# Attention products in 64x64 tiles of the array, chunks of 64 tokens, and a batch's attention woven beside mixing

## The chip, the cores and the metric

The kernel runs on one core of one Trainium2 chip. The metric is the time of one execution on the device in microseconds. Engines are named as in the profile: PE (TensorE, matrix products; PEld are its weight loads), DVE (VectorE), ACT (ScalarE), POOL (GpSimd), SP (SyncE, which issues most transfers). All arithmetic is in float32; each float32 matmul is two weight loads and two matmuls in the trace.

## The reference

A linear attention with a decaying state (4 batches, 8 heads, 768 tokens, 48 dimensions a head), then an MLP mixer over tokens and channels.

```python
# attention, per batch and head; r, k, v, w: [768, 48], u: [48]
state = 0                                     # [48, 48]
for t in range(768):
    y[t] = r[t] @ (state + outer(u * k[t], v[t]))
    state = w[t][:, None] * state + outer(k[t], v[t])
# bridge: heads side by side, x: [4, 768, 384]
h = relu(x^T @ w_tok1) @ w_tok2               # 768 -> 256 -> 768, over tokens
x = x + h^T
out = x + relu(x @ w_ch1) @ w_ch2             # 384 -> 1536 -> 384, over channels
```

The four weight matrices come as float64 and are converted on the chip from their raw bits.

## The kernel before

**Attention.** Tokens are taken in chunks of T = 128, two chunks to a unit, three units to a batch, 12 units in all. Heads lie in pairs: the d rows of one at partitions 0 to 47, of the other at 64 to 111. A unit's r is held twice (lines 84 and 92), once for each head of the pair with zeros at the other head's rows, so that one matmul with all 128 rows of k gives the products of both heads. Within a chunk the weight of token s for token t is a product of w between them; `levels` (line 173) builds it by blocks of 1, 2, 4, ... 64 tokens, 7 levels. A level is a `gram` (line 194, 8 matmuls of 128x128 into a PSUM tile of two banks) and a `join` (line 201): DVE multiplies the right halves of r, head by head (line 203, 64 partitions x 512), POOL the left halves of k (line 205) and the products of w (line 206), and DVE copies the gram's wanted entries into `pairs` under a mask (line 211). The next level's gram needs the r and k of this join.

`post` (line 222) makes the output of a unit, chunk by chunk: k is transposed (`tokens`, line 230), the term with u is made by a product of r*k with u (`own`, line 237, and line 244 on POOL), the output is accumulated from state and pairs (`result`, line 248, lines 255 and 257), and the state is carried on (`carry`, line 261: matmuls of 128x64, lines 269 to 276). Its PSUM tiles share a tag "a" with two buffers.

**Mixing.** `mixing` (line 286) is a batch's MLP: hidden (line 295, matmuls of 384 columns), back (line 301), turn (transposes, line 307), up (line 315, 256 columns, then ACT's Relu, line 317) and down (line 323, 384 columns, then DVE's addition and the transfer out).

**Weights.** `weights` (line 134) gives 28 pieces; each loads float64 bits, takes one ACT operation (line 149), five DVE operations (lines 150 to 153 and 155) and one POOL addition (line 154).

**Order.** `weave` (line 35) spreads lists of pieces over each other by cost. The loop at line 344 goes over the units: a unit's levels beside the unit before it (`post`) and, in units 1 to 3, a third of the conversions; from unit 4 on, a third of the mixing of the batch before. So batch 0's attention, all conversions and one unit of batch 1 stand ahead of the mixing of batch 0, and the last batch's mixing is alone at the end. This is the order of priority; the program's scheduler may bring forward what is ready (token products of batch 0 run from 76 us on). Loads of a unit are issued by SP (line 89).

Of the kernel before, what the change touches and what calls it, by code (L numbers as in the profile page):

```python
# [14 lines left out]
Abs = mybir.ActivationFunctionType.Abs  # L15
Relu = mybir.ActivationFunctionType.Relu

B, H, S, D = 4, 8, 768, 48
DM = H * D          # model width
T = 128             # tokens per chunk  # L20
C = S // T          # chunks per batch
UC = 2              # chunks per unit of attention work
UB = C // UC        # units per batch
NU = B * UB         # units
A = H // 2          # head pairs; heads 2a and 2a+1 lie at partitions 0 and 64
P = 64
LEVELS = 7          # block sizes 1, 2, ..., 64 halve and join a chunk of 128
COLS = UC * A * T   # columns of a unit: (chunk, pair, token)
DTOK, DCH = 256, 1536
NJ = DCH // 128  # L30
NORMAL = float(np.array(0x38100000, np.uint32).view(np.float32))  # upper word of the float64 2^-126
SEG = 256           # tokens per pass through the channel mixing


def weave(*lists):
    """Pieces (cost, f) of several lists, each list in its order and spread over the whole."""
    keyed = []
    for n, pieces in enumerate(lists):
        total, at = sum(c for c, _ in pieces), 0.0
        for i, (c, f) in enumerate(pieces):  # L40
            keyed.append(((at + c / 2) / total, n, i, f))
            at += c
    for *_, f in sorted(keyed, key=lambda e: e[:3]):
        f()


def cut_in(pieces, n):
    size = -(-len(pieces) // n)
    return [pieces[i * size:(i + 1) * size] for i in range(n)]
# [3 lines left out]
def rwkv6_then_mixer(  # L53
    ctx: ExitStack,
    tc: tile.TileContext,
    rkw: bass.AP,      # [unit, head of the pair, d, (r, k, w), (chunk pair token)]
    v: bass.AP,        # [B, S, DM]
    u: bass.AP,        # [head of the pair, d, pair]
    w_tok1: bass.AP,   # the weights are float64, as raw bits
# [3 lines left out]
    out: bass.AP,      # [B, S, DM]  # L63
):
    """The recurrence by chunks of T tokens: within a chunk, token t takes from an earlier token s
    the weight sum_d r[t, d] k[s, d] prod_{s<j<t} w[j, d]. Each pair s < t is parted by exactly one
    block size b: s lies in the left half and t in the right half of one block of 2b tokens. There
    the product is that of w from the middle to t, taken into r, and from s to the middle, taken
    into k; so only products of w over parts of (s, t) occur, whatever w holds."""
# [7 lines left out]
    xpool = ctx.enter_context(tc.tile_pool(name="xpool", bufs=2))  # L77
    ps_g = ctx.enter_context(tc.tile_pool(name="ps_g", bufs=2, space=bass.MemoryType.PSUM))
    ps_a = ctx.enter_context(tc.tile_pool(name="ps_a", bufs=2, space=bass.MemoryType.PSUM))
    ps_m = ctx.enter_context(tc.tile_pool(name="ps_m", bufs=2, space=bass.MemoryType.PSUM))  # L80

    # ---- the units' tiles: zero between the heads' rows, in r also at the other head's rows, and in
    # the weights of pairs where s >= t ----
    rs = [const.tile([128, 2, COLS], f32, name=f"r{i}") for i in range(3)]
    kws = [const.tile([128, 2, COLS], f32, name=f"kw{i}") for i in range(3)]
    pairs = [const.tile([128, UC, A, 2, T], f32, name=f"pairs{i}") for i in range(2)]
    vs = {}

    def load(i):
        for q in range(2):  # L90
            rows = slice(q * P, q * P + D)
# [6 lines left out]
    for i in range(3):  # L98
        (pool if i else dve).memset(rs[i], 0.0)
        (pool if i else dve).memset(kws[i], 0.0)  # L100
# [292 lines left out]
```

## Time and profile before

| | us |
|---|---|
| median of 3 runs (lowest, highest) | 903.5 (900.65, 904.16) |
| span of the profiled execution | 904.2 |
| PE busy (its matmuls, with overlap taken once) | 793.7, 88% |
| DVE busy | 469.1, 52% |
| POOL busy | 258.6, 29% |
| ACT busy | 104.1, 12% |

The span is that of the profiled execution, from its first to its last instruction; nothing of the run's time lies outside of it that would show beside the median. Busy time is a share over stages with different limits, so it has to be read stage by stage.

### The profile page before, as it was taken

The numbers are of one execution on the slowest core, as the hardware profiler recorded it, in microseconds if no ns is written. First come the engines' busy times: TensorE is split into PE (matmuls) and PEld (weight loads), VectorE is DVE, ScalarE is ACT, GpSimd is POOL, SyncE is SP. The second block draws the span as 40 slices with busy tenths as digits, with TensorE's granted clock in tenths as the row PEclk, the third lists the DMA queues.
The fourth block names the chain that finished last, engine by engine and source line by source line (L and its number), as shares of the span: only waits on it lengthen the run. The fifth ranks groups of instructions, "written<-read, shape, count | busy, mean of one in ns | idle before, by whom it ended". The sixth has DMA issues, their size and how long they took to land.

```text
span 904.2 us, 10421 instructions
## 1 busy us (share of the span) xinstructions
PE 793.7 (88%) x4344; PEld 648.0 (72%) x4344; DVE 469.1 (52%) x520; ACT 104.1 (12%) x249; POOL 258.6 (29%) x267
## 2 busy tenths in 40 slices
PE   2567656676689999999999999999899999999998
PEld 2566556566568997977779978777789886668674
DVE  7688697796786664443676644445656300010000
ACT  0001110110111110100011101000111010022010
POOL 8445435352443243121242431212422100000000
PEclk9976756665689999999999999999999999999999
DMA  9304324232110022001020120010000000000000
GB/s 177 78 25 96 110 75 121 70 87 88 52 36 18 19 53 62 9 9 53 9 53 19 36 67 22 10 53 9 1 1 1 1 18 9 27 1 1 18 9 26
DMA packets 14670, 36.84 MB, mean 41 GB/s; under 512 B 2208, under 2 KB 8352, under 8 KB 13472
## 3 DMA queue, kind: packets, MB, share of 16 engines
q1 hardware_dynamic: 14208, 36.18, 15.7%
q8 instruction: 34, 0.56, 0.3%
q10 hardware_dynamic: 416, 0.00, 0.1%
q14 instruction: 12, 0.10, 0.0%
HBM read 31.46 MB, written 4.72 MB: 40 GB/s over the span
## 4 chain that ended last, share of the span: by engine, by line
PE 76%; DVE 11%; POOL 8%; issue 4%; ACT 0%; POOLq 0%; DVEq 0%; ACTq 0%
PE z_ps L315 21%; PE h_ps L323 21%; PE gram L199 18%; DVE r L203 4%; PE y_ps L257 4%; PE h_ps L295 3%; PE y_ps L255 3%; POOL kw L205 3%; PE h_ps L301 2%; POOL decay L206 2%; PE own_ps L240 2%; POOL low L154 1%; DVE pairs L211 1%; DVE cut L151 1%; PE kv_ps L269 1%
## 5 line engine op out<-in xcount | busy, mean ns | idle before, releaser
L199 PE MATMUL gram<-r,kw 128*128 128x128 f32 x1344 | 210.9, 321 | 89.3 <-DVE r L203 66.7
L199 PEld LDWEIGHTS gram<-r,kw 128*128 128x128 f32 x1344 | 200.6, 232 | 101.3 <-issue 48.6
L203 DVE TENSOR_TENSOR r<-r,decay 64x512 f32<-64x512 f32 x144 | 145.4, 1010 | 124.9 <-PE gram L199 113.8
L315 PE MATMUL z_ps<-xT,wch 128*128 128x256 f32 x864 | 200.9, 386 | 0.0
L205 POOL TENSOR_TENSOR kw<-kw,decay 128x512 f32<-128x512 f32 x72 | 110.1, 1529 | 295.0 <-PE gram L199 294.9
L323 PE MATMUL h_ps<-wch,z 128*128 128x384 f32 x576 | 189.4, 487 | 0.0
L315 PEld LDWEIGHTS z_ps<-xT,wch 128*128 128x128 f32 x864 | 162.3, 193 | 21.0
L323 PEld LDWEIGHTS h_ps<-wch,z 128*128 128x128 f32 x576 | 108.5, 190 | 71.7
L211 DVE COPY_PREDICATED pairs<-mask,gram 128x1024 f32<-128x1024 uint8 x84 | 135.1, 1609 | 2.0
L325 DVE TENSOR_TENSOR o<-x,h_ps 128x384 f32<-128x384 f32 x24 | 13.3, 554 | 190.6 <-PE h_ps L323 190.6
L257 PE MATMUL y_ps<-vt,pairs 128*128 128x48 f32 x384 | 76.9, 297 | 10.1 <-DVE pairs L211 8.0
L317 ACT ACTIVATE z<-z_ps 128x256 f32<-128x256 f32 x144 | 55.3, 384 | 249.8 <-PE z_ps L315 249.8
L257 PEld LDWEIGHTS y_ps<-vt,pairs 128*128 128x128 f32 x384 | 63.5, 215 | 11.0 <-DVE pairs L211 8.3
L255 PE MATMUL y_ps<-state,r 128*128 128x48 f32 x320 | 66.3, 292 | 0.0
L255 PEld LDWEIGHTS y_ps<-state,r 128*128 128x128 f32 x320 | 55.2, 213 | 1.8 <-issue 0.6
L244 POOL TENSOR_TENSOR yd<-vt,own_sb 128x384 f32<-128x384 f32 x24 | 23.6, 982 | 98.5 <-ACT own_sb L242 98.5
L154 POOL TENSOR_TENSOR low<-low,cut 128x384 f32<-128x384 f32 (+1 forms) x28 | 34.3, 1224 | 30.4 <-DVE low L153 30.4
L301 PE MATMUL h_ps<-h,wtok 128*128 128x384 f32 x96 | 38.2, 522 | 1.3 <-DVE x L302 1.3
L295 PE MATMUL h_ps<-x,wtok 128*128 128x384 f32 x96 | 38.1, 544 | 0.0
L203 DVE TENSOR_TENSOR r<-r,kw 64x512 f32<-64x512 f32 x24 | 29.1, 1215 | 16.0 <-PE gram L199 15.6
L205 POOL TENSOR_TENSOR kw<-kw 128x512 f32<-128x512 f32 x12 | 22.5, 1877 | 45.2 <-PE gram L199 20.2
L149 ACT ACTIVATE size<-d 128x384 f32<-128x384 f32 (+1 forms) x28 | 16.9, 604 | 154.5 <-DMA d<-in_w_ch_dram 58.0
(45 smaller groups left out, 422.8 us busy)
## 6 DMA issues: line engine op xcount, KB each, us to landing
kw<-in_rkw_dram SPq DMA_DIRECT2D x24, 384.0 KB, 6.2
vt<-in_v_dram SPq DMA_DIRECT2D x12, 384.0 KB, 3.9
r<-in_rkw_dram SPq DMA_DIRECT2D x24, 192.0 KB, 3.3
d<-in_w_ch_dram SPq DMA_DIRECT2D x9, 512.0 KB, 3.6
d<-in_w_ch_dram SPq DMA_DIRECT2D x12, 384.0 KB, 3.1
out_dram<-o SPq DMA_DIRECT2D x24, 192.0 KB, 1.9
d<-in_w_tok_dram SPq DMA_DIRECT2D x3, 512.0 KB, 11.2
d<-in_w_tok_dram SPq DMA_DIRECT2D x4, 384.0 KB, 3.4
```

What stands on the lines that cost most here:

```text
L154: pool.tensor_add(low, low, cut.bitcast(f32))
L199: pe.matmul(g[:, c, a], k_[:, ts(ca, T)], right[:, :, ts(ca, nb), :], start=True, stop=True)
L203: dve.tensor_mul(right[head[q], q], right[head[q], q], wv[head[q], :, 0].unsqueeze(2).to_broadcast([P, n, b]))
L205: pool.tensor_mul(left, left, wv[:, :, 1].unsqueeze(2).to_broadcast([128, n, b]))
L211: dve.copy_predicated(out=dst, mask=masks[l].unsqueeze(1).to_broadcast([128, x, nb, b]), data=src)
L255: pe.matmul(y[:, ts(h, D)], r_[:, q, ts(c * A + a, T)], state[bt][:, a, :], start=True, stop=False)
L257: pe.matmul(y[:, ts(h, D)], at[:, c, a, q, :], vt[:, c, ts(h, D)], start=(ch == 0), stop=True)
L295: pe.matmul(ps, wtok1[:, c, ts(i, 128)], x[:, c, :], start=(c == 0), stop=(c == C - 1))
L301: pe.matmul(ps, wtok2[:, i, ts(c, 128)], h1[:, i, :], start=(i == 0), stop=(i == DTOK // 128 - 1))
L315: pe.matmul(ps, wch1[:, m, ts(jt, 128)], xT[:, m, ts(s, SEG)], start=(m == 0), stop=(m == DM // 128 - 1))
L317: act.activation(zs[s][:, jt, :], ps, Relu)
L323: pe.matmul(ps, zs[s][:, jt, ts(n, 128)], wch2[:, jt, :], start=(jt == 0), stop=(jt == NJ - 1))
```

## The change

- A chunk is 64 tokens; a unit still has 256, so each 128 tokens are two chunks j = 0, 1, and there are 6 levels instead of 7.
- r is held once ("packed"), like k and w; each has a tile of its own and is loaded by its own transfers.
- Each product of a head and a chunk uses one 64x64 tile of the array: head q gives the rows, chunk j the columns. `fours` issues the four in the order (0,0), (1,1), (1,0), (0,1). A gram is 32 matmuls of 48 rows, 64 columns of weights and 32 streamed columns. The row halves write different banks.
- The term with u goes into the first gram: its streamed columns are 32 of r and 64 of r*u (made by ACT), and the diagonal is copied into the weights. `own` falls away, and so does the addition of `yd`.
- The joins run on DVE alone, over both heads at once (112 partitions), three operations. Levels 4 and 5 are copied out of PSUM by ACT, levels 0 to 3 by DVE under a mask.
- The state is carried by chunks of 64; its PSUM tile and that of the output share one buffer. The output is copied by ACT.
- The conversions' addition moves from POOL to DVE. The conversions of the two channel weights move behind the first batch's attention, woven into the mixing of batch 0.
- Order: batch 0's attention (units 0 to 2) with the token weights' conversion; then, for each batch, its mixing with all of the next batch's attention woven through it; a unit's loads are issued at the end of the post pieces of the unit that held the tiles.

The core of the diff:

```diff
-T = 128             # tokens per chunk
-C = S // T          # chunks per batch
+T = 64
+C = S // 128
+ROWS = P + D
-LEVELS = 7          # block sizes 1, 2, ..., 64 halve and join a chunk of 128
+LEVELS = 6
...
-    rs = [const.tile([128, 2, COLS], f32, name=f"r{i}") for i in range(3)]
-    kws = [const.tile([128, 2, COLS], f32, name=f"kw{i}") for i in range(3)]
+    rs = [const.tile([128, COLS], f32, name=f"r{i}") for i in range(3)]
+    ks = [const.tile([128, COLS], f32, name=f"k{i}") for i in range(3)]
+    ws = [const.tile([128, COLS], f32, name=f"w{i}") for i in range(3)]
+    weights_at = [const.tile([128, 2, UC * A, T], f32, name=f"at{i}") for i in range(3)]
...
-            pool.tensor_add(low, low, cut.bitcast(f32))
+        dve.tensor_add(low, low, cut.bitcast(f32))
...
         def begin():
-            L["rk"] = apool.tile([128, UC, A, T], f32, name="rk")
-            rk = L["rk"].rearrange("p c a t -> p (c a t)")
-            for q in range(2):
-                dve.tensor_mul(rk[head[q]], r_[head[q], q, :], k_[head[q]])
...
+            first = L["first"] = apool.tile([128, UC, A, 2, 96], f32, name="first")
+            r5 = r_.rearrange("p (c a j t) -> p c a j t", c=UC, a=A, j=2)
+            for a in range(A):
+                act.mul(first[:ROWS, :, a, :, 32:], r5[:ROWS, :, a, :, :], u_col[:ROWS, a:a + 1])
+            act.copy(first.rearrange("p c a j t -> p (c a j) t")[:ROWS, :, :32],
+                     r_.rearrange("p (n t two) -> p n t two", t=32, two=2)[:ROWS, :, :, 1])
+
+        def fours(f):
+            for q, j in ((0, 0), (1, 1), (1, 0), (0, 1)):
+                f(q, j, slice(q * P, q * P + D), slice(j * T, (j + 1) * T))
...
+        def gram(l):
+            b = 1 << l
+            right = r_.rearrange("p (n two b) -> p n two b", two=2, b=b)[:, :, 1, :]
+            g = L["g"] = ps_g.tile([128, 2, 512], f32, name="gram")
+            for ca in range(UC * A):
+                fours(lambda q, j, rows, cols: pe.matmul(
+                    g[cols, q, ts(ca, 32)], k_[rows, ds(ca * 128 + j * T, T)],
+                    right[rows, ts(2 * ca + j, 32 // b), :], start=True, stop=True))
+
+        def pick(l):
...
+            if l < 4:
...
+                dve.copy_predicated(
...
+                return
+            g = g.rearrange("p q (x t) -> p q x t", t=32)
+            for p in range(0, 128, 2 * b):
+                n = p % T // (2 * b)
+                act.copy(at[p:p + b, :, :, n * 2 * b + b:(n + 1) * 2 * b], g[p:p + b, :, :, ts(n, b)])
 
+        def join(l, w, new):
...
+            dve.tensor_mul(left, left, wv[:, :, 1].unsqueeze(2).to_broadcast([ROWS, n, b]))
+            dve.tensor_mul(right, right, wv[:, :, 0].unsqueeze(2).to_broadcast([ROWS, n, b]))
+            dve.tensor_mul(new[:ROWS], wv[:, :, 0], wv[:, :, 1])
+
+        def first_block():
+            for c in range(UC):
+                gram0(c)
+            join(0, products[0], products[1])
+            for c in range(UC):
+                pick0(c)
+
+        def block(l):
+            gram(l)
+            join(l, products[l], products[l + 1])
+            pick(l)
...
+        def carry(c):
...
+            kv = ps_a.tile([128, 2, 512], f32, name="kv_ps", tag="a")
             for a in range(A):
+                for j, q in ((0, 0), (1, 1), (0, 1), (1, 0)):
+                    if not (last and j == 1):
+                        pe.matmul(kv[ts(q, P), j, ts(a, D)], L["kT"][ts(j, T), a, ts(q, P)],
+                                  vt[ts(j, T), c, ts(2 * a + q, D)], start=True, stop=True)
...
+        def before(c):
+            ch = half * UC + c
+            y = live[i]["y"] = ps_a.tile([128, 2, 512], f32, name="y_ps", tag="a")
...
+                for q, j in got:
+                    pe.matmul(y[ts(j, T), q, ts(a, D)], r_[q * P:q * P + D, ds((c * A + a) * 128 + j * T, T)],
+                              state[bt, 2 * ch + j][q * P:q * P + D, a, :], start=(a == 0), stop=False,
+                              skip_group_check=True)
...
+        def within(c):
...
+                for q, j in pairs:
+                    pe.matmul(y[ts(j, T), q, ts(a, D)], at[ts(j, T), q, c * A + a, :],
+                              vt[ts(j, T), c, ts(2 * a + q, D)], start=(2 * ch + j == 0 and a == A - 1), stop=a == 0,
+                              skip_group_check=True)
+            act.copy(xs[bt][:, ch, :].rearrange("p (a q e) -> p q a e", a=A, q=2),
+                     y[:, :, :A * D].rearrange("p q (a e) -> p q a e", a=A))
...
+            pieces += [(0.5, lambda c=c: tokens(c)), (0.5, lambda c=c: carry(c)), (0.5, lambda c=c: before(c)),
+                       (1.0, lambda c=c: within(c))]
+        return pieces + [(0.01, lambda: load(i + 3))]
...
+        if bt == 0:
+            pieces, ups[0] = woven(pieces, to1), woven(ups[0], to2)
...
+    emit(woven(levels(0), levels(1), conversion(wtok1, w_tok1, 2, 256)))
+    emit(woven(levels(2), post(0) + post(1), conversion(wtok2, w_tok2, 1, 384)))
+    emit(post(2))
+    for bt in range(B):
+        n = (bt + 1) * UB
+        if n < NU:
+            att = levels(n)
+            for i in range(n, n + UB - 1):
+                att += woven(levels(i + 1), post(i))
+            att += post(n + UB - 1)
+            emit(woven(att, mixing(bt)))
+        else:
+            emit(mixing(bt))
```

## Rows read from the trace of the kernel before

**Rows 1.** The page, part 1: busy us, share of the span, instructions.

```profile
PE 793.7 (88%) x4344; PEld 648.0 (72%) x4344; DVE 469.1 (52%) x520; ACT 104.1 (12%) x249; POOL 258.6 (29%) x267
```

**Rows 2.** Stages: length, busy us of PE, PEld, DVE, ACT, POOL; PE clock; DMA.

```profile
13.00:55.00 42.00, 24.57 (x121) 22.86 (x122) 30.64 (x32) 1.34 (x2) 20.15 (x27) 0.96 0.40 81
55.00:250.00 195.00, 127.71 (x706) 116.75 (x703) 157.64 (x217) 19.98 (x39) 87.40 (x81) 0.66 0.31 84
250.00:432.00 182.00, 178.75 (x1038) 146.32 (x1039) 100.19 (x96) 20.65 (x53) 53.23 (x52) 0.95 0.13 32
432.00:614.00 182.00, 179.68 (x1086) 146.29 (x1085) 98.05 (x92) 21.57 (x55) 52.11 (x52) 1.00 0.14 33
614.00:787.00 173.00, 170.68 (x976) 136.49 (x975) 66.77 (x67) 21.57 (x55) 33.32 (x31) 0.98 0.02 8
787.00:904.00 117.00, 112.13 (x427) 79.05 (x425) 7.21 (x13) 17.69 (x44) 0.00 (x0) 1.00 0.03 12
```

**Rows 3.** The chain that ended last, in order of time: start, us, what.

```profile
76.78 2.56 PE h_ps L295 x4
...
289.94 1.78 PE gram L199 x16
...
807.66 31.08 PE z_ps L315 x144
...
869.76 30.97 PE h_ps L323 x96
```

**Rows 4.** Groups by line, 432 to 614 us: busy, mean ns, idle before.

```profile
L199 PE MATMUL gram<-r,kw 128*128 128x128 f32 x336 | 42.3, 277 | 2.2 <-POOL kw L205 2.0 <-DVE r L203 0.2
...
L235 ACT COPY kT<-kT_ps 128x512 f32<-128x512 f32 x5 | 2.9, 586 | 44.0 <-PE kT_ps L233 43.8
```

**Rows 5.** Busy time of line 269 alone (PE, then PEld), count in flight in brackets.

```profile
292.94:293.00 0.06, 0.04 (x2) 0.05 (x2) 1.00 0.00 0
293.00:293.06 0.06, 0.06 (x4) 0.06 (x4) 1.00 0.00 0
293.06:293.12 0.06, 0.06 (x6) 0.06 (x6) 1.00 0.00 0
...
293.04:293.06 0.02, 0.02 (x4) 0.02 (x4) 1.00 0.00 0
```

**Rows 6.** Timeline of PE around a piece of line 269: start, us, instruction.

```profile
291.56 1.46 PE L315 MATMUL z_ps<-xT,wch 128*128 128x256 f32 x6
292.96 0.67 PE L269 MATMUL kv_ps<-vt,kT 128*64 128x48 f32 x16
293.56 2.86 PE L315 MATMUL z_ps<-xT,wch 128*128 128x256 f32 x12
```

**Rows 7.** Timeline of DVE, with one row of POOL: start, us, instruction.

```profile
59.97 0.69 DVE L203 TENSOR_TENSOR r<-r,kw 64x512 f32<-64x512 f32 x1
67.25 0.41 DVE L152 TENSOR_SCALAR scale<-cut 128x512 uint32<-128x512 uint32 x1
67.59 0.67 DVE L151 SCALAR_TENSOR_TENSOR cut<-d,cut 128x512 uint32<-128x512 uint32 x1
68.94 1.38 POOL L154 TENSOR_TENSOR low<-low,cut 128x512 f32<-128x512 f32 x1 [2.50 <-DVE low L153]
69.23 1.64 DVE L203 TENSOR_TENSOR r<-r,decay 64x512 f32<-64x512 f32 x1
78.39 1.23 DVE L211 COPY_PREDICATED pairs<-mask,gram 128x1024 f32<-128x1024 uint8 x1
666.42 0.34 DVE L276 TENSOR_TENSOR state<-state,kv_ps 128x192 f32<-128x192 f32 x1
672.62 2.45 DVE L211 COPY_PREDICATED pairs<-mask,gram 128x1024 f32<-128x1024 uint8 x1
```

**Rows 8.** Timeline of PE: the first matmuls.

```profile
12.81 3.75 PE L199 MATMUL gram<-r,kw 128*128 128x128 f32 x16 [12.81 <-DMA kw<-in_rkw_dram]
```

## What I expected, before the result was known

> **What bounds the kernel now.** I read the page first: PE is busy 88% of the span [rows 1], which alone does not say where an edit pays. So next the busy time by stage [rows 2]. From 13 us one unit's levels run alone, PE and DVE in turn (DVE busy 30.64 of 42 us, 73%). From 55 to 250 us (the rest of batch 0's attention, the weights' conversion, the first unit of batch 1) PE is busy 65% on a granted clock of 0.66, DVE 81%: this goes at the pace of DVE and of the chain through each unit's levels. From 250 to 787 us three stages follow, each one batch's mixing beside the next batch's attention: PE is busy 178.75 of 182, 179.68 of 182 and 170.68 of 173 us; these are bound by PE alone. From 787 us the last batch's mixing runs alone for 117 us.
>
> Busy time of PE overlaps itself, so the price of a matmul is taken from start to start, in the chain of work [rows 3]: 16 gram matmuls in 1.78 us are 0.111 us each, 144 of the first channel product 0.216, 96 of the second 0.323. (Each float32 matmul is two records in the trace, a weight load and a matmul each; I count records, called steps below.) A mixed stage then adds up, with 36 x 3 x 2 and 6 x 12 x 2 steps by the loops: 216 x 0.216 + 144 x 0.323 + 48 steps of token mixing with the same 384 columns at 0.323 + 18 transposes at 0.11 = 46.6 + 46.5 + 15.5 + 2.0 = 110.6 us of mixing. The 336 gram steps [rows 4] take 37.3 us; the rest of the 182 us, 34 us, are the other attention products and about 4.6 us of gaps. Attention so costs PE (182 - 110.6 - 4.6) / 3 = 22.3 us a unit in a mixed stage, and that is what the change cuts.
>
> **The change on PE.** Counted from the loops, a unit has after the change 6 levels x 32 matmuls x 2 = 384 gram steps (112 before), and 2 chunks x 3 pieces (carry, before, within) x 32 = 192 steps for state and output; 8 transposes stay. So 576 small steps stand against (1344 + 192 + 704 + 320) / 12 = 213 before, from the counts that the same loops give: the steps multiply, and all hangs on the price p of one. Nothing in the trace uses 64x64 tiles. The nearest rows are the state products (line 269), which have 64 columns and alternate between two column halves: in three stretches of 58 ns or so the count of matmuls in flight rises from 2 to 4 to 6 [rows 5], so two steps start per 58 ns, 29 ns a step instead of 111. Each half keeps a pace of its own of 58 ns (a load of half the columns), and the two run side by side. The upper bound for p is 58 ns (no two tiles side by side), the nearest measured price is 29 ns (two), the lower bound 14.5 ns (four tiles, each at its own 58 ns). The change goes through the four tiles in turn, no two of a group of four alike, and puts the two row halves into different banks of the gram's tile, so I expect four to run; I take p = 18 ns, nearer to 14.5 than to 29, the rest being allowance for issuing twice as many steps per time as any row shows. Going from full size to tiles and back is in the same rows: the 6 steps of z from 291.56 should end their turn at 292.86, the next z step starts at 293.56 [rows 6]; 0.70 us less 16 x 29 ns is 0.24 us for a piece. A unit has 12 such pieces. A unit costs PE 576 x 0.018 + 8 x 0.11 + 12 x 0.24 + 0.2 (level 0 has 96 columns instead of 32) = 14.3 us instead of 22.3. A mixed stage becomes 110.6 + 3 x 14.3 + 4.6 = 158 us.
>
> [...]
>
> **The change on DVE, ACT and POOL.** The joins' multiplication of k moves from POOL to DVE. In exchange DVE multiplies both heads at once: 512 elements took 0.69 us alone, and 1.64 us when POOL's addition ran beside it [rows 7]; POOL has only memsets left after, so I take 0.69. A unit on DVE: 6 levels x 2 x 0.69 = 8.3; the products of w of 512, 256, ... 16 elements 1.9 (scaled between 0.69 for 512 and 0.34 for 192, [rows 7]); copies under a mask: 1024 elements took 1.23 us, but 2.45 where blocks are 1 or 2 tokens [rows 7], so level 0 (256 elements at the slow pace and 512 of the diagonal, twice) 2.8, level 1 1.2, levels 2 and 3 0.7 each, 5.4; the state's multiplication and addition, 4 x 2 x 0.34 = 2.7. Sum 18.3 us. The copies of levels 4 and 5, the copy of r with u, and the output copy are now ACT's: some 8 to 10 us a unit, at 0.586 us for 512 elements [rows 4] and less for fewer, 30 us at most beside the 21.6 us that ACT has in a stage of 182 [rows 2]; hidden by PE's 158 us. A conversion of 512 columns is 2 x 0.41 + 4 x 0.68 [rows 7] = 3.6 us with the addition that comes over from POOL, one of 384 about 2.9.
>
> Each unit's loads wait at the end of its post pieces on SP, with the outputs of the mixing queued behind; the next use of the tile is a stage later, so this costs nothing as long as the post pieces aren't late.
>
> **Stage by stage.** Start to the first mixing: unit 3 and the 21 conversions of the channel weights leave this stage. DVE has 3 x 18.3 + 3 x 3.6 + 4 x 2.9 = 77 us. The first gram came at 12.81 us [rows 8]; the new one needs r times u, whose load and five ACT operations put it near 14. At 85% busy (81% in the stage of before, more since two units' levels alternate) 77 us take 91: the stage ends at 105 us (91 if DVE never waits, 120 at 73%).
> First mixed stage: 158 us of PE, but the 21 conversions (9 x 3.6 + 12 x 2.9 = 67 us of DVE) lie in its first third: there DVE has 67 + 33% of 3 x 18.3 + 3 = 88 us against 33 us of mixing and 14 of attention on PE. Attention pieces wait behind conversions on DVE and PE waits with them, up to 40 us; part is filled by mixing products that need neither, as now, where token products run between attention pieces long before their stage (in the chain they stand at 76.78 us already, [rows 3]). I take 20 us: 178 (bounds 0 and 45).
> Two more mixed stages: 158 each. Last mixing: untouched, 117 [rows 2].
> Sum: 105 + 178 + 158 + 158 + 117 = 716 us. The profiled span is 904.2 and the median of the runs 903.5, so the sum stands for the median as it is.
>
> **Rivals.**
> First, the tiles run only two at a time, as in the rows, 29 ns a step. For it: that is what was measured; against: there were only two tiles to run. A unit is 0.576 x 29 + 4.0 = 20.7 us, a mixed stage 177, the sum 105 + 20 + 3 x 177 + 117 = 773. [...]
> Second, waits take the place of PE's work: state and output products now share one buffer (the old had two), so per chunk PE's output products wait for four DVE operations (1.4 us) and the next state products for ACT's copy (0.5). At 2 us for 6 chunks a stage, 3 stages lose 36 us, and the conversions their full 45: 716 + 36 + 25 = 777. Against it: between any two such pieces lie mixing products of 1.3 us or more, and in the mixed stages of before PE was idle under 4 us.
> Third, the other side: no two tiles overlap, so that the change does not do what it says, and 576 steps go one by one at 58 ns. A unit is then 576 x 0.058 + 4.0 = 37.4 us, a mixed stage 110.6 + 112.2 + 4.6 = 227, the sum 105 + 20 + 3 x 227 + 117 = 923, slower. It turns at p = 54 ns: (903 - 242) / 3 = 220 us a stage, 35 us a unit. Against it stand the pairs of [rows 5]; for it, that rows of the array have never been split in this trace.
>
> **Chances.** Forecast (four tiles, 14.5 to 22 ns, with the bounds of the stages: 660 to 745) 0.57; first rival (any price from 22 to 29 ns) 0.22; second 0.13; third 0.06; the rest, 0.02, is anything that leaves the time where it is. About 0.5% is what a measurement of this kernel can tell from no change. Faster by more: 0.92; within: 0.02; slower: 0.06. The predicted time is the forecast's, 716 us. The low end is p = 14.5 (a unit 12.3 us), the first stage at 91 and no stall: 91 + 3 x 152 + 117 = 664, taken as 655 for what token products ahead of their stage may save; the high end takes in the first two rivals (773, 777) with the first stage at 120 instead of 105: 795 with rounding.
>
> **What would show it.** Gram pieces of 64 steps take 1.0 to 1.4 us from start to start if four tiles run, 1.9 if two, 3.7 if one. Mixed stages of about 158 us with PE busy throughout, DVE near 60 us in the second and third; DVE's multiplications of 512 at 0.69 everywhere. The first mixing begins near 105 us, with DVE over 80% busy before it, and PE's idle time in the first mixed stage is released by DVE. Wrong would be: a granted clock below 0.95 in the mixed stages, since all PE prices above are at 1.00; ACT's copies holding up PE; or a conversion stage that PE cannot fill at all.

## The result, and the profile after

The changed kernel takes 701.4 us (median of 4 runs, 700.1 to 703.5) against 902.1 us of the kernel before on the same chip: a ratio of 0.778, with a 95% interval of 0.776 to 0.781. The forecast was 716 us with a range of 655 to 795. The profiled execution took 701.8 us, of which the span is 699.7.

Part 1 of the page after (busy us, share of the span, instructions), the answer to [rows 1]:

```profile
PE 647.9 (93%) x8584; PEld 473.4 (68%) x8584; DVE 310.0 (44%) x617; ACT 177.4 (25%) x429; POOL 10.9 (2%) x36
```

PE has twice the instructions of before and 146 us less of busy time; its share has gone up, so it bounds the kernel even more than it did. The joins have left POOL.

The stages after, with the columns of [rows 2] (length, then busy us of PE, PEld, DVE, ACT, POOL; PE clock; DMA):

```profile
13.60:54.00 40.40, 31.53 (x878) 28.84 (x878) 37.02 (x71) 13.71 (x30) 0.00 (x0) 1.00 0.46 120
54.00:88.00 34.00, 25.96 (x726) 24.04 (x725) 28.87 (x66) 12.84 (x33) 0.23 (x2) 0.58 0.50 134
88.00:104.00 16.00, 15.49 (x265) 9.97 (x260) 13.54 (x27) 7.02 (x19) 0.11 (x1) 0.93 0.59 175
...
88.00:263.00 175.00, 164.82 (x2254) 116.67 (x2249) 116.24 (x239) 53.23 (x127) 0.45 (x4) 0.96 0.30 88
263.20:422.00 158.80, 156.18 (x2154) 112.03 (x2147) 56.56 (x109) 40.12 (x100) 0.22 (x2) 1.00 0.15 39
```

Before 88 us DVE is busy 92% and then 85% of the time, PE 78% and 76%. In the second mixed stage PE is busy 98%, DVE 36%. A stage runs from the first token product of one batch (line 353) to that of the next; in the timeline of PE these starts are

```profile
88.18 3.81 PE L353 MATMUL h_ps<-x,wtok 128*128 128x384 f32 x8
263.21 0.91 PE L353 MATMUL h_ps<-x,wtok 128*128 128x384 f32 x2
421.98 0.91 PE L353 MATMUL h_ps<-x,wtok 128*128 128x384 f32 x2
580.74 0.91 PE L353 MATMUL h_ps<-x,wtok 128*128 128x384 f32 x2
```

so the stages are 88.2 us to the first, then 175.0, 158.8, 158.8, and 119.0 to the end of the span. Set against the stages of before, which end at 432, 614 and 787 us [rows 2]: the end of the first mixed stage has come forward from 432 to 263 us, 169 of the 204 us that the span has lost; the second stage gave 23 us (182 to 158.8), the third 14 (173 to 158.8), and the last lost 2 of them again by where the cut lies. So most of the gain is at the front, in the part that DVE and the chain through the levels had bound. The stages don't hold quite the same work: by 432 us the kernel before had done the levels of seven units, by 263 us the changed one has done six, and the third mixed stage has three units' levels now where it had two (224 gram steps of line 199 against 336 in the second). So part of the gain at the front is a unit moved from there to the end, and the third stage's 14 us come in spite of a unit more.

The price of a step can be read from the chain of work (start, us, what), as in [rows 3]:

```profile
300.48 1.48 PE gram L209 x64
301.96 2.79 PE z_ps L373 x12
...
310.24 1.06 PE gram L227 x64
311.30 4.08 PE z_ps L373 x18
315.39 1.06 PE y_ps L331 x32
```

Sixty-four steps of a gram take 1.06 us, 16.6 ns each, where 16 full-size steps had taken 1.78. The z turns of 12 and 18 steps are 2.79 and 4.08 us: 0.215 a step, which leaves 2.79 - 12 x 0.215 = 0.21 us for the way back to full size. The last row is the exception: the product within a chunk (line 331) takes 1.06 us for 32 steps, 33 ns each.

The same two lines in three stretches of 58 ns each, the answer to [rows 5]. First line 227 alone (PE, then PEld, the number in flight in brackets):

```profile
310.24:310.30 0.06, 0.06 (x8) 0.06 (x12) 1.00 0.00 0
310.30:310.36 0.06, 0.06 (x12) 0.06 (x15) 1.00 0.00 0
310.36:310.42 0.06, 0.06 (x16) 0.06 (x15) 1.00 0.00 0
```

Then line 331:

```profile
315.39:315.45 0.06, 0.06 (x4) 0.06 (x6) 1.00 0.00 0
315.45:315.51 0.06, 0.06 (x6) 0.06 (x6) 1.00 0.00 0
315.51:315.57 0.06, 0.06 (x8) 0.06 (x6) 1.00 0.00 0
```

Four matmuls start per 58 ns in the gram, two in line 331. There the weights `at` and the streamed `vt` lie in the rows of chunk half j, and the output in the columns of the same j, so heads 0 and 1 of a half use one tile, and only the two tiles on the diagonal are ever used. In [rows 5] two started per stretch too, with two tiles in use.

### The profile page after: what moved, and what is told of

Same layout as the page of the kernel before. It is cut to its first block, busy times and chain, and to the rows that moved or that the text cites. A ratio compares the mean times of both kernels' runs of the same rounds, so it can differ in the third digit from the quotient of the medians.

```text
span 699.7 us, 18804 instructions
## 1 busy us (share of the span) xinstructions
PE 647.9 (93%) x8584; PEld 473.4 (68%) x8584; DVE 310.0 (44%) x617; ACT 177.4 (25%) x429; POOL 10.9 (2%) x36
## 4 chain that ended last, share of the span: by engine, by line
PE 78%; DVE 16%; issue 2%; DMA 2%; ACT 1%; DVEq 0%; SPq 0%; ACTq 0%
PE h_ps L381 26%; PE z_ps L373 24%; PE gram L227 7%; PE h_ps L353 5%; PE h_ps L359 4%; PE y_ps L331 4%; DVE k L252 3%; PE y_ps L318 2%; PE kT_ps L284 2%; PE gram L209 2%; PE kv_ps L296 1%; DVE scale L163 1%; DVE r L253 1%; DVE scale L162 1%; DVE cut L160 1%
## 5 line engine op out<-in xcount | busy, mean ns | idle before, releaser
L227 PEld LDWEIGHTS gram<-r,k 48*64 48x64 f32 x3840 | 75.6, 155 | 33.3 <-issue 17.1
L227 PE MATMUL gram<-r,k 48*64 48x32 f32 x3840 | 83.2, 238 | 13.5 <-DVE r L253 7.2
L252 DVE TENSOR_TENSOR k<-k,decay 112x512 f32<-112x512 f32 x36 | 24.8, 690 | 61.5 <-PE gram L227 61.3
L252 DVE TENSOR_TENSOR k<-k,w 112x512 f32<-112x512 f32 x36 | 24.7, 686 | 43.3 <-PE gram L227 42.9
L244 ACT COPY at<-gram 16x256 f32<-16x256 f32 (+1 forms) x72 | 31.2, 433 | 46.7 <-PE gram L227 33.1
L209 PE MATMUL gram<-first,k 48*64 48x96 f32 x768 | 28.0, 282 | 14.6 <-ACT first L197 13.7
L209 PEld LDWEIGHTS gram<-first,k 48*64 48x64 f32 x768 | 22.8, 158 | 20.3 <-ACT first L197 14.5
L331 PEld LDWEIGHTS y_ps<-vt,at 64*64 64x64 f32 x768 | 26.7, 145 | 9.0 <-ACT seen L324 4.5
L236 DVE COPY_PREDICATED at<-mask,gram 128x512 f32<-128x512 uint8 x36 | 32.3, 898 | 0.0
L253 DVE TENSOR_TENSOR r<-r,w 112x512 f32<-112x512 f32 x36 | 24.7, 685 | 14.1 <-ACT first L197 14.1
L331 PE MATMUL y_ps<-vt,at 64*64 64x48 f32 x768 | 29.6, 231 | 1.1 <-ACT seen L324 1.0
```

Source lines behind the costliest of these rows:

```text
L209: fours(lambda q, j, rows, cols: pe.matmul(g[cols, q, ts(a, 96)], k_[rows, ds(ca * 128 + j * T, T)], L["first"][rows, c, a, j, :], start=T ...
L227: fours(lambda q, j, rows, cols: pe.matmul(g[cols, q, ts(ca, 32)], k_[rows, ds(ca * 128 + j * T, T)], right[rows, ts(2 * ca + j, 32 // b), ...
L236: dve.copy_predicated(out=dst, data=g.rearrange("p q (m b) -> p q m b", b=b), mask=masks[l].rearrange("p x t -> p (x t)").rearrange("p (m ...
L244: act.copy(at[p:p + b, :, :, n * 2 * b + b:(n + 1) * 2 * b], g[p:p + b, :, :, ts(n, b)])
L252: dve.tensor_mul(left, left, wv[:, :, 1].unsqueeze(2).to_broadcast([ROWS, n, b]))
L253: dve.tensor_mul(right, right, wv[:, :, 0].unsqueeze(2).to_broadcast([ROWS, n, b]))
```

## Experiments

Stage lengths below are counted as above. Kernels were compared with the kernel before on the same chip, whose median was 900.4 to 902.6 us in all of these, so that differences between kernels of different groups of runs hold to about 2 us, and less well for the three kernels whose own runs lie 6 to 7 us apart (`e5_pool_join`, `e6_fused`, `e7_within_four`).

### Is it the number of tiles at work?

The theory: each tile has a pace of its own, and the gain is how many run side by side. Rival: small matmuls are cheap in themselves. Only the order of a gram's matmuls changes, not their number; in one kernel each tile's 16 steps come together (`e1_one_tile`), in the other the steps of a diagonal pair (`e2_two_tiles`).

```
-            for ca in range(UC * A):
-                fours(lambda q, j, rows, cols: pe.matmul(...))
+            for tiles in (((0, 0),), ((1, 1),), ((1, 0),), ((0, 1),)):      # e1
+            for tiles in (((0, 0), (1, 1)), ((1, 0), (0, 1))):              # e2
+                for ca in range(UC * A):
+                    for q, j in tiles:
+                        pe.matmul(...)
```

> Levels 1 to 5 of the gram issue all 8 matmuls of one 64x64 tile, then the next tile's, so neighbours never lie in different tiles. Theory (each tile has a pace of its own of 58 ns a step, and only neighbours in different tiles run side by side): a piece of 64 steps takes 3.7 us instead of 0.93 at full clock, 2.8 us more for 5 pieces of 9 units in the mixed stages = 125 us, and up to 40 us in the first stage, where PE is not alone on the path: 865 us (840 to 905), about the time of the kernel before. Rival A (PE looks far enough ahead to start the next tile's steps early, so neighbours needn't differ): under 760. Rival B (the gain of the change comes from the shorter work of DVE and the order, PE's price hardly counts): 701 to 715.

Measured 877.8 us (877.6 to 878.0), ratio 0.972 (0.967 to 0.978). From its chain of work, then its stages:

```profile
408.58 3.23 PE gram L230 x64
411.80 4.08 PE z_ps L375 x18
```

```profile
348.10:549.20 201.10, 198.95 (x2155) 150.25 (x2147) 56.57 (x109) 39.98 (x100) 0.22 (x2) 0.94 0.11 31
549.20:756.50 207.30, 205.10 (x2132) 154.50 (x2128) 53.68 (x105) 35.59 (x90) 0.00 (x0) 0.91 0.03 11
```

> Levels 1 to 5 of the gram go through two tiles in turn (the diagonal ones), then through the other two. Theory (own pace of each tile): 29 ns a step, a piece takes 1.86 us instead of 0.93, 45 pieces in the mixed stages cost 42 us, the first stage some 10: 753 us (740 to 765). That is the price of the first rival of the prediction, made real for the grams. If PE looks ahead over 16 steps or more, 701 to 710.

Measured 738.9 us (738.3 to 739.5), ratio 0.819 (0.814 to 0.823), just under the range expected. From its chain:

```profile
328.90 1.78 PE gram L230 x64
330.68 4.08 PE z_ps L375 x18
```

The same 64 steps take 3.23 us with one tile, 1.78 with two, 1.06 with four, and the kernel 878, 739 and 701. The rival falls. (Level 0 of each unit keeps its order in both kernels.)

The one-tile kernel also shows what is not the tiles. A unit costs PE 14.7 us after the change (worked out below) and 14.7 + 5 x (3.23 - 1.06) = 25.6 in this kernel, more than the 22.3 of before, and its second and third mixed stages are 19 and 34 us longer than those of before (the third with a unit more). Yet the end of its first mixed stage, at 348 us, comes 84 us earlier than the 432 of before. So of the 169 us won at the front, at least half come from the rest of the change. The join that has left POOL is 14 us in all (see below). The other candidates are a unit's levels that no longer stand ahead of the mixing, the new place of the 21 conversions, the level that fell away and the r that is held once. These were not taken apart, so what each gives isn't shown.

Both are not quite 58 and 29 ns a step (50 and 28). The trace of the two-tile kernel shows why, in stretches of 58 ns of line 230 alone around the point where the second pair begins:

```profile
329.50:329.56 0.06, 0.06 (x10) 0.06 (x6) 1.00 0.00 0
329.56:329.61 0.06, 0.06 (x12) 0.06 (x9) 1.00 0.00 0
329.61:329.67 0.06, 0.06 (x14) 0.06 (x11) 1.00 0.00 0
329.67:329.73 0.06, 0.06 (x16) 0.06 (x13) 1.00 0.00 0
```

Ten are in flight while one pair runs, sixteen where the second pair joins: for a while four tiles run, because the second pair starts before the first has finished.

The one-tile kernel is 13 us slower than its expectation's middle. The 15 grams of a stage add 15 x (3.23 - 1.06) = 32.6 us to 158.8, which makes 191; the stages took 201 and 207 at a mean granted clock of 0.94 and 0.91, and 191 divided by these is 204 and 210. In the changed kernel the same stages have 1.00, in the two-tile kernel 1.00 and 0.99. So with grams of one tile the granted clock was lower as well, 0.50 in one of the stretches below, and full-size products beside them took longer in part: 24 steps of `down` (line 383) take 9.40 us behind the gram shown here, 7.94 from 442.53 us on in the same kernel and 7.94 in the changed one (line 381, from 494.31 us). Around that gram (start, us, what; then the stretches of 1 us whose last three numbers are the granted clock and DMA):

```profile
493.43 3.39 PE gram L230 x64
496.82 9.40 PE h_ps L383 x24
```

```profile
495.00:496.00 1.00, 1.00 (x28) 1.00 (x24) 0.00 (x0) 0.00 (x0) 0.00 (x0) 1.00 0.04 8
497.00:498.00 1.00, 1.00 (x2) 0.59 (x3) 1.00 (x2) 0.00 (x0) 0.00 (x0) 0.50 0.00 0
```

The granted clock is 1.00 in the stretch from 495 us, within the gram, and 0.50 in that from 497, within the full-size product that follows, with PE busy for the whole of both.

### Does it matter which tiles are neighbours?

The edit was meant to give neighbouring matmuls the same rows more often: both column halves of one row half, then of the other.

```
-            for q, j in ((0, 0), (1, 1), (1, 0), (0, 1)):
+            for q, j in ((0, 0), (0, 1), (1, 0), (1, 1)):
```

> All grams issue the four tiles in the order (0,0), (0,1), (1,0), (1,1), so that neighbours share the row half in two of four places, instead of (0,0), (1,1), (1,0), (0,1). Theory (a tile waits only for itself): 14.5 ns a step as before, 701 us (697 to 705). [...]

Measured 700.9 us (700.0 to 702.0), ratio 0.776 (0.773 to 0.780), the same as the change. But this run doesn't show whether sharing the rows costs anything, since the edit does not do what it was meant to. Group after group, the row halves of the change run 0, 1, 1, 0, 0, 1, 1, 0 and those of this kernel 0, 0, 1, 1, 0, 0, 1, 1: in both, every second neighbour has the same rows and the others lie on a diagonal.

What decides it is in the trace of the change. The state products (line 296) go through the row halves as 0, 1, 0, 1, so that neighbours never share rows; the outputs from the state (line 318) go 0, 1, 1, 0. Both load 64 columns and stream 48:

```profile
330.27 0.61 PE kv_ps L296 x32
332.38 0.61 PE y_ps L318 x32
```

They take the same time. And of the pairs, the two column halves of the same rows in [rows 5] start two per 58 ns, just like the diagonal pair of the two-tile kernel. So sharing the rows costs nothing here.

### What do the conversions of the channel weights cost?

The prediction had a stall of 20 us from 67 us of DVE work in the first third of the first mixed stage. First they were put in front of the mixing, beside the last attention of batch 0:

```
-        if bt == 0:
-            pieces, ups[0] = woven(pieces, to1), woven(ups[0], to2)
...
-    emit(post(2))
+    emit(woven(post(2), conversion(wch1, w_ch1, 1, 512) + conversion(wch2, w_ch2, 1, 384)))
```

> The 21 conversions of the channel weights go back ahead of the first mixing, beside the last output pieces of batch 0, as in the kernel before. They are 67 us of DVE. Theory (the first stage is bound by DVE at 85 to 92% busy, so what leaves it shortens it one for one, and in the mixed stage they hide): 67 us / 0.9 = 74 us, less the some 10 of them that already run before 104 us in the changed kernel and less the 2 us that the first mixed stage loses to them: 755 us (740 to 775). Rival (PE fills the time with token products and the next batch's attention anyway, as in the kernel before): 715 to 730.

Measured 698.7 us (698.1 to 699.4), ratio 0.774 (0.770 to 0.779). Neither number came. The view of the conversions' last line (duration least/median/most, first and last start), first after, then in this kernel:

```profile
L164 DVE SCALAR_TENSOR_TENSOR wch<-size,scale x21: 541/560/692, 91.0 to 190.1; 128x384 f32<-128x384 f32 x12, 128x512 f32<-128x512 f32 x9
```

```profile
L164 DVE SCALAR_TENSOR_TENSOR wch<-size,scale x21: 545/559/693, 88.0 to 182.5; 128x384 f32<-128x384 f32 x12, 128x512 f32<-128x512 f32 x9
```

The conversions ran at nearly the same times as before the edit. Both expectations took it that they would run where the program names them; they don't, so this says nothing of their cost, and something about the prediction: they were never crammed into the first third, but spread over 100 us.

So next their work was taken away instead of moved: the 21 channel conversions become one copy each. ACT's operation for them falls away too, though the text below says that it stays (ACT has 408 instructions here, 429 in the changed kernel), so this prices both engines' work together.

```
+        if light:
+            dve.tensor_copy(dst..., hi.bitcast(f32))
+            return
```

> The 21 conversions of the channel weights keep their loads and ACT's operation, but DVE only copies the upper words (one operation of some 0.4 us instead of six, 3.4 us), so the channel weights are not the converted ones: 67 us of DVE become 8. Theory (in the changed kernel they are spread from 76 to 189 us and PE finds other work, so that little of them shows): 690 to 697 us. Rival (the prediction's step: the first mixed stage stalls some 20 us behind them): 675 to 683.

Measured 696.8 us (694.8 to 698.7), ratio 0.773 (0.766 to 0.780): 4.6 us less than the change, within what the intervals leave open. Its stages up to the second token products:

```profile
0.00:89.00 89.00, 56.58 (x1603) 51.93 (x1603) 76.61 (x154) 29.60 (x66) 10.28 (x30) 0.85 0.54 137
89.00:260.00 171.00, 164.27 (x2251) 117.18 (x2250) 65.26 (x134) 42.20 (x106) 0.45 (x4) 0.97 0.30 89
```

DVE's work in the first mixed stage goes from 116 to 65 us, and the stage only from 175 to 171. So the conversions cost some 3 to 5 us by these two runs, and not 20. What makes this stage 16.2 us longer than the second is seen without them too. PE's busy time is 8.6 us longer: the last products of batch 0 lie in it (114 steps more of lines 296, 318 and 331, 3 us of their busy time), and the rest goes with a granted clock of 0.96. And PE idles 10.2 us instead of 2.6; without the conversions it still idles 6.7.

### Where is DVE on the path?

Useless multiplications of 112 x 512 (0.67 to 0.69 us each), one for each level of a unit, either in batch 0 (18 of them, 12.4 us) or in the units of the three mixed stages (54, 37 us):

```
+            if i < UB:                 # e9; in e10: if i >= UB
+                dve.tensor_mul(idle..., left, right)
```

> Each of the 18 joins of batch 0 (units 0 to 2, ahead of the first mixing) does one more multiplication of 112 x 512 on DVE, whose result is not used: 18 x 0.69 = 12.4 us of DVE in the first stage. Theory (that stage goes at the pace of DVE): 12 us more, 713 us (709 to 716). Rival (it goes at the pace of PE's grams at half clock, or of the round trips between the engines): 701 to 706.

Measured 709.7 us (707.6 to 711.7), ratio 0.786 (0.781 to 0.791): 8.3 us more than the change. The first token product starts 9.5 us later:

```profile
97.73 2.70 PE L356 MATMUL h_ps<-x,wtok 128*128 128x384 f32 x6
```

> The same useless multiplication in each of the 54 joins of units 3 to 11, in the mixed stages: 37 us more of DVE. Theory (PE bounds the mixed stages, DVE has room): 701 to 705 us. Rival (the joins' chain sets the pace of attention there): 715 to 738.

Measured 705.5 us (705.0 to 706.0), ratio 0.781 (0.777 to 0.785), half a microsecond above the theory's range. The stages are 178.9, 159.1 and 159.2 us: 3.9 more in the first mixed one, 0.4 at most in the others, with 11 to 12 us more of DVE's work in each. From these single executions, two thirds of what was added to DVE came through in the time at the start, a third in the first mixed stage, and next to nothing after it.

DVE isn't alone at the start, though. The time up to the first token product in the changed kernel, with two tiles at a time and with one, where DVE does the same work:

```profile
0.00:88.00 88.00, 57.50 (x1602) 52.88 (x1602) 76.61 (x154) 30.06 (x67) 10.27 (x30) 0.84 0.54 138
0.00:97.80 97.80, 72.60 (x1603) 68.71 (x1603) 77.41 (x154) 29.76 (x66) 10.27 (x30) 0.84 0.46 124
0.00:132.40 132.40, 109.41 (x1602) 105.71 (x1602) 77.67 (x154) 30.20 (x67) 10.27 (x30) 0.84 0.35 92
```

Of 15.1 us more of PE's busy time 9.6 came through, of 51.9 us 44. So the start goes at the pace of the chain of grams and joins, on both engines in turn.

### What did moving the join of k to DVE bring?

One line puts the multiplication of k back on POOL, as it was before the change.

```
-            dve.tensor_mul(left, left, wv[:, :, 1]...)
+            pool.tensor_mul(left, left, wv[:, :, 1]...)
```

> The joins' multiplication of k is put back on POOL, all else as changed. It takes 0.69 us off DVE in each of 72 joins and gives POOL 72 operations of 1.05 to 1.5 us. Theory (POOL and DVE hold each other up when both read two operands, as 0.69 against 1.64 us showed in the kernel before): DVE's multiplications of r rise to 1.0 us or more, the first stage gains nothing or loses some us, the mixed stages are bound by PE and stay: 699 to 712 us, centre 703. Rival (the first stage is bound by DVE's own work, so 18 x 0.69 = 12 us less of it shorten it): 689 to 692.

Measured 715.3 us (714.3 to 720.9), ratio 0.794 (0.790 to 0.798), 14 us more, and above both ranges. Groups of its POOL and of its DVE by line (busy us, mean ns, idle before):

```profile
L252 POOL TENSOR_TENSOR k<-k,decay 112x512 f32<-112x512 f32 x36 | 58.9, 1636 | 196.5 <-PE gram L227 125.6 <-issue 54.9 <-DVE wch L164 10.8
L252 POOL TENSOR_TENSOR k<-k,w 112x512 f32<-112x512 f32 x36 | 55.3, 1535 | 225.2 <-PE gram L209 113.3 <-PE gram L227 83.9 <-issue 14.1
```

```profile
L253 DVE TENSOR_TENSOR r<-r,decay 112x512 f32<-112x512 f32 x36 | 28.6, 794 | 65.4 <-PE gram L227 65.4
L253 DVE TENSOR_TENSOR r<-r,w 112x512 f32<-112x512 f32 x36 | 25.3, 702 | 61.5 <-PE gram L227 45.5 <-ACT first L197 16.0
```

And who waited for POOL on PE (us in all, times, longest):

```profile
PE kT_ps L284 <- POOL k L252: 10.4, 7, 1.9
PE gram L227 <- POOL k L252: 8.2, 7, 2.6
```

On POOL the multiplication takes 1.5 to 1.6 us instead of 0.69. DVE is busy 18 us less in this kernel and the time is longer: the start and the first mixed stage are 92.7 and 181.5 us, 4.5 and 6.5 more, and each of the two later stages 1.8 more. With PE waiting for POOL, that speaks for the length of a unit's chain, level after level, and not DVE's load alone.

The theory that the two engines hold each other up holds in part. The 72 multiplications were 49.5 us on DVE, and its busy time fell by 18 us only, since its other operations take longer in this kernel: line 162's of 512 elements 838 ns on average instead of 683, the multiplications of r 702 and 794 instead of 685 and 684. But those of r are on average far from the 1.64 us of [rows 7], and from the 1.0 us or more that was expected. It isn't confined to operations that read two operands either: in the kernel before, line 150, which reads one, took 1.72 us beside POOL's multiplication at 122.5 us (1.67 us), against 0.41 in the median.

### A faster version

Two things in the trace are still for the taking. The product within a chunk can use all four tiles if the second head writes the other half of the output rows, which takes three output copies of ACT instead of one. Line 318, which writes the same buffer, and the copy `seen` change with it (not shown):

```
...
-                    pe.matmul(y[ts(j, T), q, ts(a, D)], at[ts(j, T), q, c * A + a, :],
+                    pe.matmul(y[ts(j ^ q, T), q, ts(a, D)], at[ts(j, T), q, c * A + a, :],
```

> The product of weights and values (within) uses only the two diagonal tiles in the changed kernel: its rows and its columns are both the chunk's half. Here the second head of each pair writes to the other half, so that all four tiles are used; ACT then takes the output in three copies instead of one. Theory (own pace per tile): a piece of 32 steps takes 0.47 us instead of 0.93, 18 pieces in the mixed stages: 8 us less, 692 to 695 us. Rival (ACT's longer copies hold the shared PSUM buffer and PE waits): 700 to 704.

Measured 690.3 us (685.5 to 692.6), ratio 0.764 (0.761 to 0.768). From its chain:

```profile
304.34 0.61 PE y_ps L333 x32
```

0.61 us instead of 1.06, and 156.2 us a stage instead of 158.8: six such pieces are 6 x 0.45 = 2.7. Three stages make 8 us of the 11 that the kernel gained, which is more than expected; the others lie at the start and in the first mixed stage, and were not taken apart (the runs of this kernel differ by 7 us).

And pieces of different units can follow each other, which saves 12 of the 36 ways back to full size in a stage:

```
...
+            att = one[:2] + two[:2] + [both(x, y) for x, y in zip(one[2:], two[2:])]
...
```

> In the mixed stages two tile pieces of different units are issued one behind the other where they can be (grams of two units; grams of the third beside state and output pieces of the first), so that PE goes from full size to tiles 24 times a stage instead of 36. Theory (going there and back costs 0.24 us, measured beside line 269 before): 12 x 0.24 x 3 = 8.6 us less, 693 us (690 to 697). Rival (neighbouring grams wait for the same DVE and ACT, and PE waits with them): 701 to 708.

Measured 693.3 us (689.2 to 695.5), ratio 0.768 (0.764 to 0.771). From its chain:

```profile
307.96 2.00 PE gram L227 x128
309.96 6.73 PE z_ps L373 x30
```

128 steps take 2.00 us, 14.7 ns for each of the second 64; the stage is 155.1 us, 3.7 less, which is 12 x (0.21 + 0.12) = 4.0 with the 0.12 us that the first steps of a piece cost more.

> Both edits that shortened PE's work at once: pieces issued one behind the other (24 instead of 36 a stage) and four tiles in the product of weights and values. Theory (both save PE's own time, in different places, and PE is the bound of the mixed stages): the savings add, 701.4 - 8.1 - 11.1 = 682 us (679 to 686). Rival (with less work on PE the joins' chain on DVE and ACT comes next): 688 to 693.

Both together measured 686.0 us (684.3 to 687.7), ratio 0.759 (0.756 to 0.762), at the upper end of what was expected. The second and third mixed stages are 152.7 and 152.8 us, so both gains are there in full; the first is 174.1 us, where the four-tile kernel had 168.7. If the fused order costs something where the chain of a unit is short of time, it should be left out there:

> The four-tile version of the within product in all units, as in the kernel with that edit alone (690.3 us), and the tile pieces of different units back to back only from the second batch on, so not in the first mixed stage. Theory: the fused order costs something only where VectorE is loaded, in the first mixed stage (174.1 us with it, 168.7 without), and takes 3.6 us off each of the second and third mixed stages (156.2 to 152.7). The start should be as in the four-tile kernel (84 us), the first mixed stage near 169, the two others near 152.7, the end 117: 690.3 - 7.0 = 683 us (680 to 686). Rival: the gain that was missing when both edits were made together is not a matter of the stage, and this one gives 686 to 690 like the two others.

Measured 683.8 us (682.8 to 684.7), ratio 0.758 (0.756 to 0.760), the lowest median of all, though its interval overlaps that of the kernel with both edits everywhere. Its stages:

```profile
0.00:85.60 85.60, 54.48 (x1606) 49.65 (x1606) 77.31 (x155) 30.75 (x70) 10.28 (x30) 0.86 0.55 140
85.60:256.70 171.10, 160.04 (x2254) 112.58 (x2246) 115.49 (x238) 57.06 (x137) 0.45 (x4) 0.98 0.31 91
256.70:409.40 152.70, 150.96 (x2136) 108.67 (x2128) 55.90 (x109) 42.38 (x108) 0.22 (x2) 1.00 0.15 41
```

The time came out as the theory has it, its stage only in part: 171.1 us is halfway between 168.7 and 174.1. The profiled execution of the four-tile kernel was the fastest of its four runs, 4.8 us below its median, so its 168.7 may have been a lucky one. That the fused order costs 2 us in the first mixed stage is likely, not shown.

## Why the prediction was right, and where its steps were off

**The price of a step.** Right, and the theory behind it: four tiles, each at its 58 ns. The price was taken at 18 ns; it is 14.7 in a long piece, close to the lower bound of 14.5, plus about 0.12 us that each piece costs at its beginning. The allowance for issuing so many steps was not needed. A gram piece of 64 takes 1.06 us, inside the 1.0 to 1.4 that was named for four tiles. That the 58 ns are a load of half the columns fits the kernel before: with 128 columns of weights 16 steps took 1.78 us with 128 streamed columns [rows 3] and 1.72 with 48 (line 257, from 626.59 to 628.31 us), so 111 and 108 ns a step.

**"The change goes through the four tiles in turn."** Wrong for one of the four kinds of pieces: line 331 goes through two. Its 64 steps a unit cost 33 ns instead of 18, 1.0 us a unit. The four-tile version gave that back (1.06 to 0.61 us a piece).

**The unit and the stage.** From the rows after: 5 grams x 1.06 + 1.48 (level 0) + 4 pieces of state x 0.61 + 2 x 1.06 (within) + 12 x 0.21 + 8 x 0.11 = 14.7 us, against 14.3 in the prediction: price too high, line 331 too low, and by luck the two nearly cancel. 110.6 + 3 x 14.7 + 4.6 = 159.3; the second and third mixed stages are 158.8. Here the sum holds, with one term of unclear source: the 4.6 us of gaps are worked out from no row, and PE idles 2.6 us in the second mixed stage.

**Start and first mixed stage.** Here the sum is off, and only here: 283 us predicted to the end of the first mixed stage, 263.2 measured. The attention of batch 0 is over when it was forecast, its last output copy ending at 99.8 us and PE having a stage's work alone from 104. The forecast added up DVE's work alone. 12.4 us more of that came through by two thirds, but a higher price of the grams came through there in the same way, so that the 105 fitted although half of the chain was left out of the sum. Line 353, though, began at 88.2, below the bound of 91: its products add up chunk by chunk and needn't wait for the last. The 24 steps of line 353 that were done by 104 are 24 x 0.323 = 8 us of mixing ahead, and unit 3's first grams about 2 us more. The other part is the stall: from 104 on, 158 - 10 = 148 us of PE's work took 159, so 11 us were lost where 20 were taken. And these 11 are for the most part not what the prediction named: the conversions cost some 3 to 5 us, running from 91 to 190 us and not in a third of the stage; the rest goes with a granted clock of 0.96, which is above the 0.95 that the prediction had set as a sign of being wrong, and with short waits. Of PE's idle time, 6.4 us were ended by DVE, as forecast, and 3.7 by ACT. The largest waits are small (us in all, times, longest, from 88 to 265 us):

```profile
PE h_ps L359 <- ACT xT L366: 1.7, 3, 0.6
PE gram L227 <- DVE r L253: 1.7, 1, 1.7
PE y_ps L318 <- DVE state L306: 1.5, 2, 0.9
```

Where the 4 us of PE's idle time come from that this stage has above the later ones even without the conversions was not tracked down.

**The last stage** is untouched: 117.0 us from 582.7, as before.

**DVE and ACT.** DVE in the second mixed stage has 56.6 us (60 forecast), and the multiplications of 512 elements take 684 to 693 ns, as forecast from the row that had no POOL beside it. ACT has 40.1 us and PE waits 0.3 us for it.

**The rivals.** Two tiles at a time is a real case, and the kernel built so gave 739 us; the rival's 773 had the stall of 20 us and a start of 105 in it, which are not there either, and every small step at 29 ns, where that kernel slows only the grams of levels 1 to 5. Waits in place of work: in the second mixed stage PE waits 1.0 us for the state (line 306), where the rival had 12 a stage. A wait that was not priced is the two-column copy `seen` (line 324), which parts the two uses of the output's buffer: it holds up weight loads of line 331 for 4.5 us in the whole kernel, and its matmuls for 1.0. No overlap: that kernel was built for the grams, and it was still 2.8% faster than before rather than slower, since the state and output products kept their overlap and tiles overlap a little even when taken one after the other (50 ns a step, not 58).

## What to carry to other kernels

Small matmuls are best priced from start to start, per tile, and then divided by the number of tiles that are really in use (64 gram steps took 3.23, 1.78 and 1.06 us here with one, two and four): list rows and columns of every kind of piece, since one that looks the same may use only the diagonal (line 331, 33 ns a step). Each turn from full size to tiles and back costs about 0.3 us here, so pieces are worth joining where nothing waits for them. Where the program names a piece of work need not be where it runs (the last of the conversions' final operations began at 190.1 us here, and at 182.5 when they were named ahead of the mixing); before a stall is forecast from its place, see whether the trace of before shows such work spread out, and take the work away rather than move it to learn its price.

## What the runs showed of the hardware that was not expected

- Tiles that share their rows run side by side as freely as tiles that don't: 32 steps take 0.61 us where every second neighbour shares them (line 318) and where none does (line 296).
- A later tile's matmuls start while an earlier tile still has some to run: 10 in flight in the pair, 16 where the second pair joins, and 50 ns a step instead of 58 with one tile at a time.
- With one tile at a time the granted clock of the mixed stages was 0.94 and 0.91, with four 1.00, though PE was busy 99% of the time in the one and 98% in the other: the full-size products beside them, unchanged, became slower in part (24 steps of `down` in 9.40 us, 7.94 with four).
